# One order of work for another in an adaLN block with dilated window attention and a token-mixing MLP: loads on two queues, idle matmuls and the first transposes

## The chip, the core and the metric

The kernel runs on one NeuronCore of one Trainium2 chip. The metric is the device time of one execution in microseconds (us), the median over several runs. Five engines take part: PE (TensorE, matmuls; PEld is its weight loads), DVE (VectorE), ACT (ScalarE), POOL (GpSimd) and SP (SyncE, which here only issues DMAs). Each engine takes its own instructions strictly in the order in which the program gives them, so a row that waits holds up everything behind it on that engine.

## What is computed

x is 2048 tokens by 512 channels (bfloat16). Cut to what matters, the reference is:

```python
mod = silu(c) @ w_mod                      # 6 rows of 512: sa ca ga sb cb gb
h = layernorm(x) * (1 + ca) + sa
qkv = h @ wqkv                             # 32 heads of 16
# every token s attends to s, s-2, s-4, ... s-14 (8 keys, earlier than 0 masked)
x = x + ga * (softmax(q . k / 4) . v) @ wo
h = layernorm(x) * (1 + cb) + sb
h = layernorm(h)                           # first step of the MLP
u = gelu(h.T @ w1 + b1)                    # mixes tokens: 2048 -> 1792, per channel
y = u @ w2 + b2                            # 1792 -> 2048
x = x + gb * y.T
```

## The kernel before

The 2048 tokens are 16 tiles of 128. The attention half works on five chunks of 2, 4, 4, 4 and 2 tiles (SIZES). In each chunk the layer norm statistics are taken on DVE (one bn_stats) or on ACT (two passes with an accumulator), the rows are normalised, turned to channels on partitions (by PE in chunks 0 and 1, by a transposing DMA in chunks 2 to 4), and multiplied by wqkv. DVE forms the products of q with the eight shifted k (`qk`, four per chunk), PE sums them over the heads' channels (`red`), then follow maximum, exponent and sum, and DVE forms the products with v (`pv`, four per chunk), which PE sums (`pvacc`). PE multiplies by wo and adds x with an identity matmul; second and third layer norm follow (`ln2`, `aff`, `ln3`, `h3`). The first MLP product (`mlp1`) accumulates over the 16 token tiles, and so can begin on the early tiles while later chunks are in attention; its partial sums are parked in SBUF (`park`) and brought back by a PE identity matmul (`inj`) or by a DVE addition. After GELU, `mlp2` gives the 16 output tiles one after the other; `fin` on DVE and a store end each.

**Who sets the order.** The kernel builds a list of some 790 named operations with their dependences, and the string ORDER names them in the order in which they are issued. Behind a colon stands the engine for operations that have a choice (`:a` ACT, `:d` DVE, `:p` POOL, `:s` SP); for matmuls `:q` splits one into four 32-column ones and `:n` leaves the identity matmul out (DVE adds instead). `fill:64` is a piece of idle matmuls: 64 units, that is 16 matmuls of the identity by itself with 512 columns, and one of 128 columns for each unit left over; nobody reads their result. Token by token, `schedule` picks engine, PSUM bank and buffer.

**Names that the change and the steps below touch.** All of them are in the one kernel function.

- `ident` and `consts` (POOL): the identity matrix, and the group and mask constants. PE's first matmul needs the identity.
- `act_table` (ACT): loading the activation table. `ld_c`, `cps`, `silu_exp`, `silu_dve`: the condition row c is loaded, turned to a column by PE, and silu is taken on ACT and DVE, giving `sc`.
- `ld_x1`, `ld_x0`, `ld_x_1_2`, `ld_x_1_4`: token tiles of chunk 0 (one each) and the two tile pairs of chunk 1.
- `ln1s`, `ln1v`, `rstd1`, `nb1`, `n1`: statistics, variance, reciprocal deviation, offset and normalised rows of the first layer norm.
- `modcols1` (16 one-column matmuls of w_mod by sc) and `a1col` (DVE): the columns 1 + ca, the "scale columns". `hT0`, `hT1` (ACT or DVE): copies of the transposed tokens out of PSUM, multiplied by `a1col`. `tr0_0`, `tr1_0`, `tr1_2` are the transposes in front of them.
- `qkv0_02` and following: the first products with wqkv; `modcols0`, `sab`, `qvb0`, `qvb_cp0`: the offsets that sa brings to q; `ev0`: eviction of q and k; `qk0`: the first products of q and k on DVE.

Of loads that may go by SP's or ACT's queue, the helper is:

```python
QS = (("sp", nc.sync), ("act", nc.scalar))
def dma2(out_ap, in_ap, nbytes, writes, name):
    return G.add_any([(n_, 0.5, lambda q_=q_: q_.dma_start(out_ap, in_ap)) for n_, q_ in QS], writes=writes, name=name, ...)
```

The kernel's own numbers such as `0.5` are planning costs; with ORDER written out they decide nothing.

Of the kernel before, what the change touches and what calls it, by code (L numbers as in the profile page):

```python
# [196 lines left out]
qkv0_00 qvb0 wsc0_0:p ev0_10:a ld_b2 ld_wo1 hT1_1:d qkv1_00 ln1s11:d ln1s10:d ln1s13:d qkv1_10:q ln1v11 ln1v10
qvb_cp0:a ev0_00:a ln1s12:a ev0_02:d qkv1_13 ld_wqkv2 qkv0_20 ln1v13 qk0_3 qk0_2 ev1_13:a qk0_0 qvb1 ln1v12 qkv0_22:q
ld_wrow0 red0_0 ev1_00:a qkv1_03:q ev1_10:a qk0_1 red0_1 red0_2 red0_3 mask qvb_cp1:a ev0_20:a ev0_22:a wsc1_2:p
halo_v1:a qk1_0 ev1_03:a wsc1_3:a qkv1_11:q ld_wmod2 wsc2_3:a modrow0 ld_b1 mrows0:a ev1_11:a ld_wrow2 qkv1_02 max0  # L200
wsc0_2:p ld_wo0 n1_7:p sub0 rstd1_3 qkv1_01 ld_wo2 exp0 qkv1_12:q wsc1_1:p esum0:q qk1_3 red1_0 ev1_01:a qk1_1
ev1_02:a biascols n1_6:p ld_wrow1 rcp0 smB0 ev1_12:a ld_x_4_14 ln1s14:a qkv1_22 qk1_2 a2_0_2:a xt6 ld_wrow3 modrow1
red1_1 a2_0_1:a n1_9:p wsc2_0:d ln1s15:a ln1v14 nb1_3 n1_11:a qkv1_23:q mrows1 qkv1_21 ev1_21:a red1_2 red1_3 xt8
ev1_23:a fill:1 n1_10:p qkv1_20 ev1_20:a ev1_22:a qkv2_13 qkv2_10 wsc0_1:p vd0_2 ev2_13:a ln1v15 vd0_1 max1 sub1
qkv2_00 exp1 a2_0_0:s a2_0_3:s pv0_1 vd0_0 pv0_0 st_row0 pv0_2 qkv2_03 esum1:q ld_wo3 pvacc0_0 vd0_3 halo_v2:p
biascols_cp:a pvacc0_1 pv0_3 pvacc0_2 pvacc0_3 ev2_10:a ev2_00:a qk2_0 n1_13:a n1_12:a ld_row0 woq_s rcp1 smB1
# [5 lines left out]
qkv3_02:q ev3_00:a pv1_3 ev3_02:a pvacc1_0 ev3_20:a qkv3_01:q ev3_01:a qkv3_11:q xt14 ld_row1 n2_1:p vd2_3 pvacc1_1
smB2 aff0 qk3_0 vd2_1 fill:1 vd2_0 oev1_0:a oev1_1:a pvacc1_3 ev3_11:a qk3_1 qkv3_23:q oev1_3:a a2_2_2:s ln3s1:a
qkv3_03:q wo4 a2_2_1:s qk3_2 a2_2_0:s ev3_03:a ev3_23:a x1_4:a ln2q4:a wo2 x1_2:a a2_2_3:s red3_0 wo3:q x1_3:a ln2q3:a
qkv3_21:q ev3_21:a wo5 red3_1 pv2_3 x1_5:a vd2_2 qk3_3 qkv4_20:q red3_2 qkv4_22 red3_3 qkv4_12 fill:18 ln2q5:a
ld_w1_0_512 ln2q2:a ln2m2 pv2_0 pvacc2_0 vd3_0 ev4_20:a ln3s0:a ln3v0 ev4_12:a rstd2_2 ev4_22:a ln3v1 qkv4_02 oev2_0:a
ln2m4 rstd2_4 nb2_2 n2_2:a max3 sub3:q exp3 pvacc2_3 oev2_3:a qkv4_10:q pv2_2 vd3_2 esum3 nb2_4 pv2_1 vd3_1 n2_3:p
ld_w1_0_0 n2_5:a rcp3 smB3 pvacc2_2 fill:14 a2_3_0:s a2_3_1:s a2_3_3:s n2_4:a qkv4_00:q oev2_2:a rstd3_0 aff2 pvacc2_1
oev2_1:a wo6 wo9 wo7 aff4 nb3_0 ln3s2:d ev4_02:a ln3s3:a ln3v3 h3_1:p wo8 a2_3_2:s ev4_00:a ln3v2 ld_w2_0 ln3s4:d
rstd3_2 nb3_2 x1_9:a ln3s5:a h3_0:p mlp1_0_6_0:q x1_7:a ln3v4 x1_8:a h3_3:d mlp1_0_1_0 h3_2:d mlp1_0_6_2 mlp1_0_1_2  # L220
pv3_1 mlp1_0_5_0:q ln3v5 ev4_10:a ld_w1_0_896 x1_6:a mlp1_0_3_0:q mlp1_0_3_2:q ln2q7:a pvacc3_1 rstd3_4 mlp1_0_5_2:q
# [15 lines left out]
ld_w2_4 mlp1_1_0_10 ln3v14 ln3v12 rstd3_12 h3_11:a mlp1_1_6_10 inj1_5:n mlp1_1_5_6 mlp1_1_5_10 rstd3_14 mlp1_1_1_10
aff15 nb3_12 ln3s15:d ln3v15 h3_12:p nb3_14 park1_0:+ h3_13:p rstd3_15 nb3_15 inj1_2:n mlp1_1_2_6 ld_w1_1_896 h3_14:p
h3_15:a ld_w1_2_0 park1_1:+ mlp1_1_2_10 park1_2:+ mlp1_1_7_10 park1_3:+ park1_4:+ park1_5:+ mlp1_1_8_10 mlp1_1_10_10
park1_6:+ padd1_7 padd1_10 gelu10 padd1_8 mlp1_1_9_10 padd1_9 gelu9 mlp1_2_4_11 mlp1_2_4_14 mlp1_2_1_11 mlp1_2_1_14  # L240
padd2_1 padd2_4 gelu7 mlp1_2_0_11 mlp1_2_0_14 padd2_0 gelu0 mlp1_2_2_11 gelu4 gelu8 mlp1_2_2_14 ld_w1_1_1408
mlp1_2_3_11 mlp1_2_3_14 padd2_3 gelu3 ld_w1_2_640 mlp1_2_6_11 padd2_6 gelu6 padd2_2 gelu2 mlp1_2_5_11 mlp1_1_11_10
padd1_11 mlp1_2_5_14 padd2_5 gelu1 gelu11 mlp1_1_12_10 ld_w2_5 ld_w2_7 mlp1_1_13_10 gelu5 mlp2_0_0 padd1_12 gelu12
mlp2_0_0b ld_w2_2 ld_w2_9 ld_w2_13 ld_w2_11 padd1_13 gelu13 mlp2_0_0c mlp2_6_0 mlp2_4_0 gsc fin0_0 st_out0_0 fin4_0
st_out4_0 mlp2_8_0 fin8_0 mlp2_3_0 fin3_0 mlp2_2_0 fin2_0 st_out2_0 mlp2_1_0 fin1_0 mlp2_7_0 st_out3_0 fin6_0
st_out6_0 fin7_0 mlp2_10_0 fin10_0 st_out7_0 mlp2_11_0 mlp2_5_0 st_out1_0 fin5_0 st_out5_0 mlp2_14_0 fin11_0
# [829 lines left out]
```

## Time and profile before

| what | us |
|---|---|
| time, median of 3 runs | 201.56 (201.33 to 201.79) |
| the profiled execution's own time | 202.11 |
| span of its profile | 200.4 |
| PE busy / DVE busy / ACT busy in the span | 191.0 / 159.6 / 128.6 |

The span runs from the first to the last instruction of the program; 1.7 us of the execution lie outside it. Every row of the profile carries line 142, the wrapper that issues all instructions, so rows are told apart by the tiles they write and read ("psS<-hT,wst" is a product of tokens with raw wqkv, "big<-q_sb,k_f" a `qk`, "big<-a2sb,vD" a `pv`, "psL<-big,group" a `red`). A timeline row gives start, length, engine, operation and tiles, the count of instructions merged in it, and in brackets the idle time before it and what ended that. Lengths of PE matmuls are from start to modelled end and overlap; their pace is read from the starts or from long rows.

### The profile page before, as it was taken

The numbers are of one execution on the slowest core, as the hardware profiler recorded it, in microseconds if no ns is written. First come the engines' busy times: TensorE is split into PE (matmuls) and PEld (weight loads), VectorE is DVE, ScalarE is ACT, GpSimd is POOL, SyncE is SP. The second block draws the span as 40 slices with busy tenths as digits, with TensorE's granted clock in tenths as the row PEclk, the third lists the DMA queues.
The fourth block names the chain that finished last, engine by engine and source line by source line (L and its number), as shares of the span: only waits on it lengthen the run. The fifth ranks groups of instructions, "written<-read, shape, count | busy, mean of one in ns | idle before, by whom it ended". The sixth has DMA issues, their size and how long they took to land.

```text
span 200.4 us, 4572 instructions
## 1 busy us (share of the span) xinstructions
PE 191.0 (95%) x1818; PEld 95.8 (48%) x1836; DVE 159.6 (80%) x241; ACT 128.6 (64%) x306; POOL 18.6 (9%) x45
## 2 busy tenths in 40 slices
...
GB/s 161 341 355 350 176 240 127 160 56 185 300 143 321 220 167 194 176 112 311 64 310 257 36 184 196 160 186 234 338 244 298 85 26 52 27 52 52 174 52 52
DMA packets 53889, 35.95 MB, mean 179 GB/s; under 512 B 24428, under 2 KB 50668, under 8 KB 53868
## 3 DMA queue, kind: packets, MB, share of 16 engines
...
q8 instruction: 14, 0.23, 0.5%
...
HBM read 22.55 MB, written 2.10 MB: 123 GB/s over the span
## 4 chain that ended last, share of the span: by engine, by line
PE 69%; DVE 22%; issue 4%; DMA 1%; ACT 1%; ACTq 0%; DVEq 0%
PE psS L142 67%; DVE big L142 14%; PE psL L142 3%; DVE st L142 2%; DVE h L142 2%; DMA c_t<-in_c_dram 1%; DVE mv L142 1%; ACT h L142 1%; DVE lsb L142 1%; DVE m L142 1%; DVE nb L142 0%; ACTq L142 0%; DVE woq L142 0%; DVE hT L142 0%; ACT rb L142 0%
## 5 line engine op out<-in xcount | busy, mean ns | idle before, releaser
L142 PEld LDWEIGHTS <-wst 128*128 128x128 bf16 (+1 forms) x536 | 34.9, 101 | 33.7 <-issue 4.0
L142 PE MATMUL psS<-h,wst 128*128 128x512 bf16 (+1 forms) x333 | 50.3, 380 | 0.5 <-issue 0.3
L142 DVE TENSOR_TENSOR big<-q_sb,k_f 128x4096 bf16<-128x4096 bf16 (+1 forms) x20 | 36.6, 1859 | 0.4 <-ACT q_sb L142 0.4
L142 DVE TENSOR_TENSOR big<-a2sb,vD 128x4096 bf16<-128x4096 bf16 (+1 forms) x20 | 36.5, 1860 | 0.2
L142 PE MATMUL psS<-hT,w_qkv 128*32 128x512 bf16 (+3 forms) x360 | 29.7, 346 | 0.0
L142 DVE SCALAR_TENSOR_TENSOR h<-psS,bcol,rows_bc 128x512 f32<-128x512 f32 (+2 forms) x17 | 12.1, 710 | 22.1 <-PE psS L142 20.6
L142 PEld LDWEIGHTS <-w_qkv 128*32 128x32 bf16 (+1 forms) x402 | 19.4, 109 | 17.8 <-issue 4.4
L142 PE MATMUL psS<-gT,big 128*128 128x512 bf16 x110 | 24.7, 379 | 0.1
L142 PEld LDWEIGHTS <-big 128*128 128x128 bf16 x144 | 12.0, 97 | 13.5
L142 ACT ACTIVATE junk<-xx 128x512 bf16<-128x512 bf16 x26 | 16.3, 627 | 3.3 <-DVE xx L142 1.4
L142 PE MATMUL psS<-woq,o_sb 128*32 128x512 bf16 (+1 forms) x107 | 15.7, 380 | 0.9 <-ACT o_sb L142 0.6
L142 ACT ACTIVATE gT<-psS,bcol 128x512 bf16<-128x512 f32 x14 | 9.0, 685 | 8.1 <-DVE psS L142 8.0
L142 POOL TENSOR_SCALAR h<-xx,rs,nb 128x512 bf16<-128x512 bf16 x9 | 6.9, 766 | 75.6 <-DVE nb L142 36.5
L142 DVE TENSOR_TENSOR psS<-psS,gT 128x512 f32<-128x512 f32 x14 | 9.3, 695 | 5.0 <-PE psS L142 5.0
L142 ACT ACTIVATE h<-xx,nb,rs 128x512 bf16<-128x512 bf16 x16 | 12.4, 808 | 0.5 <-DVE nb L142 0.4
L142 PEld LDWEIGHTS <-ident 128*32 128x32 bf16 (+1 forms) x137 | 7.0, 102 | 10.5 <-issue 5.9
L142 PE MATMUL psS<-ident 128*128 128x512 bf16 (+1 forms) x35 | 10.6, 450 | 1.4 <-POOL epscol L142 1.4
L142 PE MATMUL psS<-hT,wst 128*32 128x512 bf16 (+2 forms) x110 | 11.7, 352 | 0.1
L142 DVE TENSOR_TENSOR h<-h,xx 128x512 bf16<-128x512 f32 (+2 forms) x17 | 11.1, 653 | 0.6
L142 DVE TENSOR_TENSOR h<-h,rows_bc 128x1024 bf16<-128x1024 bf16 (+2 forms) x16 | 10.9, 689 | 0.4
L142 DVE BATCH_NORM_STATS2 st<-xx 128x6 f32<-128x512 bf16 x12 | 7.9, 680 | 3.9 <-DMA xx<-in_A_x_dram 3.8
L142 ACT ACTIVATE v_sb<-psS,qvb 128x512 bf16<-128x512 f32 (+1 forms) x20 | 11.0, 595 | 0.0
...
## 6 DMA issues: line engine op xcount, KB each, us to landing
...
```

The costliest lines, as they stand in the source:

```text
L142: r = fn(*a, **k)
```

## The change

The load of c gets the choice of queue that the token loads have, and ORDER is another list. Of the list, the head, the tokens spoken of below and the end are shown; the engines chosen for other operations change in 29 places.

```diff
-    add("act", 0.55, lambda: nc.scalar.dma_start(c_t[:], c[0].rearrange("(t p) -> t p", p=P)), writes=["c_t"],
-        name="ld_c", lat=2.0)
+    dma2(c_t[:], c[0].rearrange("(t p) -> t p", p=P), D * 4, ["c_t"], "ld_c")
...
-ident ld_x_1_2:a halo0 ld_c consts ld_x1:s ld_x0:s ld_x_1_4:s act_table ln1s3:d fill:4 cps ld_wmod1 silu_exp silu_dve
-fill:64 ln1s1:a ln1s2:a ln1s0:d ln1v1 ld_x_2_8 ln1v0 ln1s4:d ld_wqkv0 rstd1_0 nb1_0 n1_1:a fill:4 ln1v4 n1_0:p ln1s5:d
-ln1v2 ln1v5 ln1v3 rstd1_1 nb1_1 ld_x_2_6 modcols1 n1_2:d n1_5:d ln1s8:a a1col wsc0_3:p n1_4:d tr0_0 hT0_1:a hT0_3:a
-n1_3:d hT0_0:a fill:13 hT0_2:a ld_wqkv1 ld_wmod0 ln1s9:d ld_x_3_10 ln1s6:d tr1_0 tr1_2 hT1_2:a ln1v6 qkv0_02 ln1v9
+act_table ld_x1:s consts ld_c:a ident fill:13 ld_x_1_2:a cps silu_exp silu_dve ld_x0:s ln1s0:d ln1v0 ld_x_1_4:s
+ld_wmod1 ln1s1:a fill:70 ln1v1 rstd1_0 nb1_0 n1_0:p ln1s4:d ln1s5:d ln1s3:d ln1s2:a ln1v2 n1_1:a tr0_0 ln1v5 fill:7
+ld_x_2_6 ld_wqkv0 ln1v3 ln1v4 rstd1_1 nb1_1 n1_2:a n1_3:d n1_5:d modcols1 a1col wsc0_3:p hT0_1:a n1_4:d tr1_0 ld_wqkv1
+wsc0_0:p tr1_2 hT0_2:a hT0_0:a ln1s7:d ld_x_2_8 ln1s6:d ln1v6 wsc0_1:d wsc1_0:p fill:6 halo0 ld_wmod0 ld_x_3_10
+hT0_3:a qkv0_02 hT1_3:a ln1s9:d qkv0_10 hT1_0:a qkv0_12 modcols0 ln1s8:d hT1_1:a wsc1_1:p qkv0_00 ld_x_3_12 ld_wqkv2
...
-fill:1 ... fill:1 ... fill:18 ... fill:14          (pieces of idle matmuls in the attention half)
+fill:1 ... fill:9
...
-inj1_5:n
+inj1_5
...
-... mlp2_15_1 fin15_1 st_out15_1 mlp2_15_2 fin15_2 st_out15_2
+... mlp2_15_1 mlp2_15_2 fill:24 fin15_1 st_out15_1 fin15_2 st_out15_2
```

More of the change, by code (lines that the diff above doesn't have):

```diff
@@ L197 @@
[L197 to L206, printed above, removed]
@@ L212 @@
[L212 to L221, printed above, removed]
@@ L237 @@
[L237 to L246, printed above, removed]
@@ L247 @@
-st_out10_0 st_out11_0 ld_w2_15 fpre mlp2_9_0 mlp2_13_0 fin14_0 st_out14_0 st_out8_0 mlp2_12_0 fin9_0 st_out9_0 fin13_0
-st_out13_0 mlp2_15_0 fin12_0 st_out12_0 fin15_0 st_out15_0 mlp2_15_1 fin15_1 st_out15_1 mlp2_15_2 fin15_2 st_out15_2
+act_table ld_x1:s consts ld_c:a ident fill:13 ld_x_1_2:a cps silu_exp silu_dve ld_x0:s ln1s0:d ln1v0 ld_x_1_4:s
+ld_wmod1 ln1s1:a fill:70 ln1v1 rstd1_0 nb1_0 n1_0:p ln1s4:d ln1s5:d ln1s3:d ln1s2:a ln1v2 n1_1:a tr0_0 ln1v5 fill:7
+ld_x_2_6 ld_wqkv0 ln1v3 ln1v4 rstd1_1 nb1_1 n1_2:a n1_3:d n1_5:d modcols1 a1col wsc0_3:p hT0_1:a n1_4:d tr1_0 ld_wqkv1
@@ new lines @@
+wsc0_0:p tr1_2 hT0_2:a hT0_0:a ln1s7:d ld_x_2_8 ln1s6:d ln1v6 wsc0_1:d wsc1_0:p fill:6 halo0 ld_wmod0 ld_x_3_10
+hT0_3:a qkv0_02 hT1_3:a ln1s9:d qkv0_10 hT1_0:a qkv0_12 modcols0 ln1s8:d hT1_1:a wsc1_1:p qkv0_00 ld_x_3_12 ld_wqkv2
+ln1v7 ev0_10:a ln1v9 ln1v8 rstd1_2 sab:a qvb0 hT1_2:d qkv1_13:q ev0_12:a nb1_2 n1_9:a ln1s10:d ln1s13:d qvb_cp0:d
+ev0_02:a qkv1_00:q ln1s11:d ld_wrow0 ln1v10 ev0_00:a ln1s12:a ev1_00:a qkv1_03:q ln1v11 ln1v13 qkv0_20 qkv1_10
+ld_wrow2 ev1_03:a ld_wrow3 qvb1 n1_7:a ld_wo0 ld_wmod2 qk0_2 qk0_0 n1_6:p red0_0 qkv0_22:q qk0_3 qk0_1 red0_1
@@ new lines @@
+qkv1_11:q wsc0_2:p ev1_10:a red0_2 qk1_0 ld_b2 ld_wrow1 n1_8:p red0_3 mask ld_wo3 ln1v12 wsc2_2:a ld_x_4_14 max0
+ev1_13:a qk1_3 qkv1_01 xt6 qvb_cp1:a ev0_22:a ev0_20:a wsc1_2:a vd0_2 ev1_11:a sub0 exp0 vd0_3 fill:1 xt8 qkv1_02
+ev1_01:a esum0:q qk1_1 modrow1 rcp0 modrow0 ev1_02:a qkv1_12 mrows0:a st_row0 wsc2_0:a smB0 a2_0_3:s ev1_12:a qk1_2
+a2_0_0:s qkv1_21 wsc2_1:a ld_wo1 rstd1_3 a2_0_2:a a2_0_1:a ln1s14:a qkv1_22:q qkv1_23:q wsc1_3:a nb1_3 ev1_22:a
+n1_10:p mrows1 ln1s15:d ev1_23:a ln1v14 red1_0 red1_1 red1_2 red1_3 qkv1_20 vd0_1 qkv2_00 vd0_0 ld_row0 ev2_00:a max1
@@ new lines @@
+pv0_3 sub1 qkv2_11:q qkv2_10 exp1 esum1 n1_13:p halo_v1:a ev1_20:a qkv2_12 pv0_2 pvacc0_2 pv0_1 ev1_21:a rcp1 ev2_10:a
+ev2_11:a wsc2_3:a ev2_12:a qkv2_03:q ev2_03:a pv0_0 ld_b1 pvacc0_0 smB1 ln1v15 qkv2_01:q ev2_01:a ld_wo2 n1_11:p xt10
+pvacc0_3 pvacc0_1 oev0_0:a qkv2_02:q ev2_02:a qkv2_13:q halo_v2:p vd1_3 oev0_2:a qkv2_23 qk2_0 qkv2_22 n1_12:a woq_s
+wo0:q ev2_22:a qk2_1 rstd1_4 a2_1_3:s red2_0 ev2_13:a x1_0:a qk2_2 ln2q0:a vd1_2 wo1:q x1_1:a qk2_3 a2_1_2:s red2_1
+qkv2_21:q xt12 qkv3_11:q ln2q1:a ln2m0 nb1_4 qkv3_02:q a2_1_0:s a2_1_1:s pv1_2 ev3_11:a ev2_21:a rstd2_0 nb2_0 n1_15:a
@@ new lines @@
+red2_2 red2_3 ev3_02:a st_row1 qkv3_10:q ev3_10:a pvacc1_2 oev1_2:a ev2_23:a vd1_0 max2 qkv3_13 qkv2_20 sub2:q ld_row1
+n1_14:a vd1_1 halo_k3:a ev2_20:a qkv3_00:q exp2 pv1_0 pvacc1_0 oev1_0:a qkv3_12:q qkv3_21:q vd2_0 pv1_3 pvacc1_3
+ev3_00:a esum2 qkv3_03:q ev3_21:a xt14 n2_1:p pv1_1 n2_0:a aff0 ev3_13:a pvacc1_1 oev1_3:a vd2_2 qkv3_01:q ev3_03:a
+qk3_0 oev1_1:a wo3:q wo4:q rcp2 wo5 smB2 ev3_12:a qkv3_20:q ln3s0:a qkv4_10 qk3_3 x1_4:a ev3_01:a qk3_1 vd2_3 qk3_2
+ln3s1:a x1_5:a ln2q4:a wo2 ld_w1_0_512 ln2q5:a a2_2_2:s x1_3:a ln2q3:a x1_2:a a2_2_0:s qkv3_23:q red3_0 a2_2_1:s
@@ new lines @@
+halo_v3:a qkv4_02 ln2q2:a a2_2_3:s ev3_20:a red3_1 ln2m4 red3_2 rstd2_4 ev3_23:a pv2_3 vd2_1 qkv4_22:q ev4_22:a
+ld_w1_0_896 nb2_4 n2_5:a qkv3_22 ev3_22:a ln2m2 rstd2_2 qkv4_20:q halo_v4:p biascols biascols_cp:a pv2_0 ld_w1_0_0
+red3_3 vd3_1 ev4_02:a vd3_3 nb2_2 vd3_2 n2_2:a max3 fill:9 pvacc2_0 sub3 ev4_10:a pvacc2_3 n2_4:a pv2_2 exp3 qkv4_12
+pv2_1 ev4_20:a vd4_0 ld_w2_2 esum3 rcp3 pvacc2_2 smB3 a2_3_2:s oev2_2:a a2_3_3:s qkv4_00 ev4_12:a oev2_3:a oev2_0:a
+ln3v0 pvacc2_1 oev2_1:a wo7 a2_3_1:s n2_3:p ln3v1 ev4_00:a wo6 aff2 rstd3_0 aff4 wo9 wo8 nb3_0 ln3s2:d a2_3_0:s
@@ new lines @@
+ln3s3:a x1_6:a h3_1:p h3_0:p mlp1_0_5_0 mlp1_0_6_0 ln3v3 ln3v2 rstd3_2 ln3s4:d x1_7:a nb3_2 h3_3:a ln3s5:a ln3v4
+h3_2:d x1_9:a mlp1_0_1_0 ln2q6:a x1_8:a pv3_1 ln3v5 mlp1_0_1_2 rstd3_4 mlp1_0_6_2 mlp1_0_3_0 vd3_0 pv3_0 mlp1_0_3_2:q
+pvacc3_1 oev3_1:a mlp1_0_5_2:q nb3_4 mlp1_0_0_0:q mlp1_0_2_0 mlp1_0_2_2:q mlp1_0_0_2:q qk4_2 pv3_2 h3_5:a h3_4:a
+mlp1_0_2_4:q mlp1_0_0_4:q mlp1_0_1_4:q mlp1_0_3_4:q pv3_3 mlp1_0_6_4:q ln2q7:a ln2q8:a park0_0:a park0_1:a ln2q9:a
+ln2m6 park0_2:a ld_w2_3 mlp1_0_5_4:q pvacc3_2 oev3_2:a pvacc3_0 qk4_3 park0_3:a mlp1_0_8_0:q mlp1_0_8_2:q pvacc3_3
@@ new lines @@
+rstd2_6 nb2_6 oev3_0:a qk4_0 mlp1_0_4_0:q mlp1_0_4_2:q mlp1_0_4_4:q oev3_3:a wo12:q ld_w1_0_1152 wo13:qn red4_0 n2_9:a
+vd4_2 n2_8:a n2_6:a n2_7:d qk4_1 red4_1 x1_12:a red4_2 red4_3 park0_4:a mlp1_0_7_0:q park0_5:a aff6 ln2q12:a max4
+mlp1_0_10_0 mlp1_0_10_2 ln3s8:d ln3s6:d ln3s7:a ln3v7 wo11 x1_11:a park0_6:a ln3s9:d mlp1_0_7_2 mlp1_0_7_4 ln3v6 ln3v8
+ln3v9 sub4 exp4 rstd3_6 mlp1_0_8_4 x1_13:d nb3_6 ln2q13:a mlp1_0_9_0 mlp1_0_9_2 ld_w1_0_1408 vd4_1 mlp1_0_12_0
+mlp1_0_12_2 mlp1_0_10_4 h3_6:p esum4 rcp4 vd4_3 ln2m12 h3_7:d h3_9:d smB4 rstd2_12 wo10:n a2_4_3:s h3_8:d ln2q11:a
@@ new lines @@
+nb2_12 a2_4_1:a n2_13:p a2_4_2:a mlp1_0_9_4 x1_10:d n2_12:a ln2q10:d ln2m10 aff12 mlp1_0_12_4 mlp1_0_7_6 mlp1_0_8_6
+park0_7:a mlp1_0_9_6 mlp1_0_11_0 mlp1_0_10_6 rstd2_10 mlp1_0_12_6 a2_4_0:s park0_8:a park0_9:a nb2_10 inj1_5
+mlp1_0_11_2 n2_11:a ln3s13:a pv4_2 mlp1_0_11_4 park0_10:a pv4_0 pvacc4_0 mlp1_0_11_6:q n2_10:a ld_w1_0_1664 pv4_1
+pvacc4_1 oev4_0:a pvacc4_2 mlp1_0_13_0:q pv4_3 pvacc4_3 inj1_3:qn aff10 ln3s11:d park0_11:a mlp1_0_13_2 mlp1_0_13_4
+ld_w1_1_0 oev4_2:a wo14 x1_14 wo15 mlp1_0_13_6 ld_w1_1_640 mlp1_1_3_6 mlp1_1_5_6 ln3s10:a ln3v10 ln3v11 rstd3_10
@@ new lines @@
+park0_12:a ln2s14 ln2v14 x1_15 inj1_6:qn mlp1_1_6_6 rstd2_14 ld_w1_1_896 nb2_14 n2_14:p inj1_0:n ln2s15 mlp1_1_0_6
+inj1_1:n mlp1_1_1_6 ln2v15 aff14 ln3s12:a nb3_10 rstd2_15 nb2_15 h3_10:a mlp1_1_3_10 park0_13:a n2_15:p mlp1_1_5_10
+mlp1_1_6_10 ln3s14:d ln3v14 mlp1_1_1_10 ln3v12 ln3v13 rstd3_12 aff15 nb3_12 h3_13:p mlp1_1_0_10 rstd3_14 h3_11:p
+ln3s15:d ld_w2_0 h3_12:a ln3v15 park1_0:+ ld_w1_2_0 nb3_14 rstd3_15 nb3_15 inj1_4:n mlp1_1_4_6 park1_1:+ mlp1_1_4_10
+inj1_2:n mlp1_1_2_6 mlp1_1_2_10 ld_w1_1_1408 h3_15:d park1_2:+ h3_14:a mlp1_1_10_10 mlp1_1_8_10 ld_w2_4 park1_3:+
@@ new lines @@
+park1_4:+ park1_5:a park1_6:+ fpre mlp1_1_9_10 padd1_9 mlp1_1_7_10 padd1_7 ld_w1_2_640 mlp1_2_1_11 gelu9 gelu7
+mlp1_2_1_14 ld_w2_1 mlp1_2_4_11 padd2_1 mlp1_2_0_11 gelu1 padd1_8 gelu8 mlp1_1_11_10 padd1_11 gelu11 padd1_10 gelu10
+mlp1_2_0_14 mlp1_2_4_14 padd2_4 mlp1_2_2_11 mlp1_2_2_14 padd2_2 mlp1_2_3_11 ld_w2_5 padd2_0 mlp1_2_3_14 padd2_3 gelu4
+mlp1_2_6_11 padd2_6 gelu3 gelu2 mlp1_2_5_11 mlp1_2_5_14 padd2_5 mlp1_1_12_10 padd1_12 gelu0 gelu5 mlp1_1_13_10
+padd1_13 gelu6 gelu12 mlp2_0_0 mlp2_0_0b gelu13 mlp2_1_0 fin1_0 gsc mlp2_2_0 fin2_0 mlp2_0_0c mlp2_4_0 ld_w2_7 ld_w2_9
```

26 lines of the change are left out of this document (5 added, 21 removed).

## The prediction, made before the changed kernel ran

> **What bounds the kernel now.** I read the page first, then the chain of work that ended last, then busy time by stretches, and then the timeline of the first 26 us, where most of the change lies. The page and, below it, pieces of the chain (start, length, what):
>
> ```profile
> PE 191.0 (95%) x1818; PEld 95.8 (48%) x1836; DVE 159.6 (80%) x241; ACT 128.6 (64%) x306; POOL 18.6 (9%) x45
> ```
> ```profile
> 1.33 2.60 DMA c_t<-in_c_dram
> ...
> 3.98 7.09 PE psS L142 x34
> ...
> 11.10 0.16 DVE a1col L142
> 11.26 1.02 DVE h L142 x2
> ...
> 56.29 10.16 PE psS L142 x141
> ...
> 69.33 5.71 DVE big L142 x3
> ...
> 102.95 1.14 DVE big L142
> ...
> 144.85 10.74 PE psS L142 x49
> ...
> 197.36 0.29 DVE h L142
> ```
>
> The chain begins with the load of c, runs over PE's idle matmuls, a1col and two normalised rows, goes to and fro between PE and DVE until 104 us, and is PE's alone from there to the end. The long piece gives PE's pace: 10.74 / 49 = 0.219 us for a matmul of 512 columns. The stretches (length, then busy PE, PEld, DVE, ACT, POOL) say which of the two is the limit:
>
> ```profile
> 18.80:104.10 85.30, 83.12 (x1197) 42.45 (x1198) 84.28 (x86) 79.88 (x191) 5.23 (x8) 1.00 0.67 194
> 104.10:197.10 93.00, 92.39 (x490) 43.77 (x499) 62.95 (x118) 34.67 (x82) 4.57 (x6) 1.00 0.54 148
> ```
>
> Between its first `qk` (18.80) and the end of its last (104.1) DVE is idle for 85.30 - 84.28 = 1.02 us in all. So the time is: start of the first `qk`, plus DVE's work up to the last `qk`, plus PE's work behind it, plus a fixed end. I work out what the change does to each.
>
> **Part 1, the start.** The rows of the timeline that carry it:
>
> ```profile
> 0.81 0.20 POOL L142 MEMSET ident<- 128x128 bf16 x1 [0.29 <-POOLq L1060]
> 0.82 0.48 ACTq L142 DMA_DIRECT2D xx<-in_A_x_dram  x1
> 1.32 0.10 POOL L142 MEMSET epscol<- 128x1 f32 x1
> 1.33 0.61 ACTq L142 DMA_DIRECT2D c_t<-in_c_dram  x1
> 1.52 0.12 POOL L142 MEMSET group<- 128x32 bf16 x1
> 1.98 1.28 ACT L142 ACT_TABLE_LOAD   x1 [1.98 <-issue]
> 2.94 0.29 POOL L142 TENSOR_SCALAR_AFFINE_SELECT nident<-nident 128x128 bf16<-128x128 bf16 x1
> 3.98 0.18 PE L142 MATMUL psS<-ident,c_t 4*128 4x4 bf16 x1 [1.94 <-DMA c_t<-in_c_dram]
> 4.10 6.58 PE L142 MATMUL psS<-ident 128*128 128x512 bf16 x17
> 4.27 0.62 ACT L142 ACTIVATE junk<-xx 128x512 bf16<-128x512 bf16 x1
> 7.90 0.81 ACT L142 ACTIVATE h<-xx,nb,rs 128x512 bf16<-128x512 bf16 x1 [0.23 <-DVE nb L142]
> 8.77 0.15 PEld L142 LDWEIGHTS <-ident 128*128 128x128 bf16 x1 [0.28 <-issue]
> 9.19 0.15 PEld L142 LDWEIGHTS <-ident 128*128 128x128 bf16 x1 [0.28 <-issue]
> 9.62 0.57 PEld L142 LDWEIGHTS <-ident 128*128 128x128 bf16 x3 [0.28 <-issue]
> 10.52 0.54 PE L142 MATMUL psS<-sc,big 128*128 128x1 bf16 x16
> 10.92 0.61 PE L142 MATMUL psS<-ident,h 128*128 128x128 bf16 x8
> 11.10 0.16 DVE L142 TENSOR_SCALAR a1col<-psS 128x4 f32<-128x4 f32 x1 [0.66 <-PE psS L142]
> 11.57 1.57 ACT L142 ACTIVATE hT<-psS,a1col 128x256 bf16<-128x256 bf16 x4 [0.73 <-PE psS L142]
> 12.07 1.28 PE L142 MATMUL psS<-ident,h 128*128 128x128 bf16 x16
> 13.19 2.78 PE L142 MATMUL psS<-hT,wst 128*128 128x256 bf16 x24
> ```
>
> Before: the idle matmuls come every 0.43 us until about 9.6 and at double pace from there; they end at 10.5, and the first product with wqkv starts at 13.19.
>
> After, in order. POOL makes the constants (1.52 to 2.94 + 0.29 = 3.23, so 1.71 us) ahead of the identity (0.81 to 1.42, so 0.61): 0.81 + 1.71 + 0.61 = 3.13 for PE's first matmul, where it was 1.43. ACT loads its table first: c is issued at 0.82 + 1.28 = 2.10 where it was 1.33, and lands 2.65 later (1.33 to 3.98) at 4.75. The new piece of 13 units (3 wide matmuls and a narrow one, 1.4 us) hides that wait. The token pair that was first on ACT's queue now starts at about 2.7; its first reader comes at 7.2, so 4 us of other work hide the later load. Behind c's column, 70 units are 17.5 wide matmuls from 4.87 on.
>
> The double pace came 9.6 - 4.1 = 5.5 us into steady matmuls. By the same distance it comes at 3.13 + 5.5 = 8.65: (8.65 - 4.87) / 0.427 = 8.9 slow ones, then 8.6 x 0.219 = 1.9 us: end at 10.55, as before (10.5). What follows is longer. The first transposes (0.45) and the piece of 7 (one wide, three narrow: 0.38) now stand ahead of modcols1 (10.92 - 10.52 = 0.40, and 0.18 until a1col): a1col starts at 10.55 + 1.41 = 11.95, where it was 11.10. Its copies cannot begin earlier by the swap, for `hT0` multiplies by a1col; and `n1_4` stands behind a1col on DVE, so the transposes of chunk 1 wait for it as well: 11.95 + 0.16 + 0.37 = 12.5, 16 transposes 0.9, the piece of 6 0.33: first product at 13.75. ACT agrees: a1col's end 12.1 + 1.57 = 13.7. That is **+0.56**. Behind it the kernel runs the same six steps to the first `qk` (three products, modcols0, product, qvb0), so 18.80 becomes 19.35.
>
> The ends: if the pace doubles at a fixed 9.6, 11.1 slow and 6.4 fast matmuls end at 11.0, +1.0. If it doubles much sooner, other things hold the start: ACT reaches its first statistics 0.77 later (4.27 to 5.04, with c), the row written by 7.90 + 0.81 = 8.71 ends at 9.5, a normalised row of chunk 1 follows at 10.7 to 11.5 on ACT, and the four copies end at 13.1: -0.1. I keep +0.56, range -0.1 to +1.0.
>
> [...]
>
> **Part 2, DVE from the first `qk` to the last.** The order of `qk` and `pv` hardly changes. Between these two points three operations differ: one weight scaling (0.35) and one `h3` row (0.41) leave DVE, and one bn_stats (0.68) comes:
>
> ```profile
> L142 DVE BATCH_NORM_STATS2 st<-xx 128x6 f32<-128x512 bf16 x12 | 7.9, 680 | 3.9 <-DMA xx<-in_A_x_dram 3.8
> L142 DVE TENSOR_SCALAR h<-h,rs,nb 128x512 bf16<-128x512 bf16 x5 | 1.9, 409 | 0.0
> L142 DVE TENSOR_SCALAR w_qkv<-h,a1col 128x512 bf16<-128x512 bf16 x1 | 0.3, 346 | 0.0
> ```
>
> 0.68 - 0.76 = **-0.08**. Waits are unknown: at best all 1.02 us of idle time go, at worst a new one as large comes (PE takes one more product of chunk 1, qkv1_11, four wide matmuls or 0.9 us, ahead of the matmuls that the maximum of chunk 0 waits for); I take 0 and keep both ends. The pieces of idle matmuls in this part shrink from 34 units to 10:
>
> ```profile
> 76.61 1.14 PE L142 MATMUL psS<-ident 128*128 128x512 bf16 x6
> ...
> 82.34 0.93 PE L142 MATMUL psS<-ident 128*128 128x512 bf16 x5
> ```
>
> At PE's pace 24 units are 6 wide matmuls, 1.3 us. They stand at the maximum of chunk 3, where PE waits for DVE; I cost them at nothing, as DVE's work is the same; -1.3 is the end if PE were last there.
>
> **Part 3, PE behind the last `qk`.** The same matmuls in another order, and inj1_5 on PE again where DVE added: one wide matmul, **+0.22**. The `:q` marks that come and go cost nothing: split or whole, the columns are the same. Two late weight blocks (ld_w2_11, ld_w2_15) stand behind stores on SP's queue, but five or more output tiles ahead of their readers, 14 x 0.219 = 3.1 us each. fill:24 (6 wide, 1.3 us) comes behind the last real matmul, while the last store is out:
>
> ```profile
> 196.38 0.94 PE L142 MATMUL psS<-woq,wst 128*128 128x128 bf16 x14
> ```
>
> It ends near 198.6, and the span at 200.4; without that cover it would cost at most 1.3.
>
> **Sum.** 0.56 - 0.08 + 0.22 = +0.7. The profiled execution took 202.11 (span 200.4 and 1.7 around it), so 202.8 by its own measure; it lay 0.55 above the median of the runs, 201.56, and so **202.2** as a median.
>
> **Rivals.**
>
> - *Idle time in the middle is won* (faster). If PE, not DVE, is last between 69 and 104 us, the 24 units count: 201.56 + 0.56 + 0.22 - 1.3 = 201.0; with the early start of part 1, 200.4. For it: PE is 83.1 of 85.3 us busy there, and the chain lies with PE for 10.16 us from 56.29. Against: the chain is DVE's from 69 to 104. It decides if DVE's idle time falls well below 1.02. Chance 0.26.
> - *The change does little of what it says.* c and one pair are on ACT's queue in both kernels, and a large idle piece is there in both; if the start is held by ACT (-0.1) and the rest repeats, 201.6. [...] Chance 0.20.
> - *Late clock or a new wait.* Pace doubling at 9.6 as before (+1.0 for the start), or DVE waiting some 0.5 us for evictions in chunks 0 and 1: 201.56 + 1.0 + 0.2 to 0.7 = 202.9. Against: steady matmuls begin 0.85 earlier. Chance 0.18.
> - The forecast, 202.2: chance 0.36.
>
> A measurement of this kernel tells about 0.2%, 0.4 us, from no change. Faster 0.26, same 0.20, slower 0.36 + 0.18 = 0.54. The range, 200.7 to 203.1, goes to most of the first rival and past the third; 0.2 stay outside.
>
> **What would show it.** a1col's start near 11.95 and the first wqkv product near 13.75 (13.1 and 14.2 are the ends); first `qk` near 19.35; DVE busy about 84 us from there to its last `qk`, idle time near 1; then 93 us of PE. It is wrong if the first `qk` starts at 18.8 or earlier, if DVE's idle time goes to near 0, or if PE shows waits behind 104 us that it did not have.

## The result, and the profile after

The changed kernel took 203.34 us (median of 6 runs, 202.48 to 203.93), the kernel before 201.49 on the same chip (6 runs, 201.25 to 201.79). The ratio is 1.0088, with a 95% interval of 1.0058 to 1.0117: slower by 1.85 us. The prediction said 202.2 and 200.7 to 203.1: the right direction, but 0.7 where 1.85 came.

The profiled execution took 202.48, with a span of 200.4. It was the quickest of the six; the other spans were 200.7 to 201.8. Its page shows almost the same busy times as before, with one block of instructions more (queue 8: 15 packets and 0.25 MB, so 16 to 17 KB each; before, 14 and 0.23 MB):

```profile
PE 192.1 (96%) x1890; PEld 96.8 (48%) x1890; DVE 158.6 (79%) x240; ACT 127.3 (64%) x302; POOL 19.3 (10%) x45
...
q8 instruction: 15, 0.25, 0.5%
```

Pieces of the chain of work that ended last (start, length, what). It no longer begins with the load of c: POOL's constants and then the identity start it and release PE at 3.09; then come DVE's statistics and a row on ACT.

```profile
2.74 0.29 POOL ident L142
...
3.09 1.70 PE psS L142 x5
...
5.67 0.61 DVE st L142
...
7.42 1.79 DVE st L142 x3
...
10.36 0.82 ACT h L142
...
11.54 10.77 PE psS L142 x157
```

The start, from the timeline (start, length, engine, operation, tiles):

```profile
0.81 1.28 ACT L142 ACT_TABLE_LOAD   x1 [0.81 <-PEq L1060]
0.84 0.57 ACTq L142 DMA_DIRECT2D c_t<-in_c_dram  x1
1.44 0.41 ACTq L142 DMA_DIRECT2D xx<-in_A_x_dram  x1
4.59 0.18 PE L142 MATMUL psS<-ident,c_t 4*128 4x4 bf16 x1
6.81 2.73 PEld L142 LDWEIGHTS <-ident 128*128 128x128 bf16 x13 [0.28 <-issue]
9.56 0.61 PE L142 MATMUL psS<-ident,h 128*128 128x128 bf16 x8
11.01 0.15 DVE L142 TENSOR_SCALAR a1col<-psS 128x4 f32<-128x4 f32 x1
12.66 2.78 PE L142 MATMUL psS<-hT,wst 128*128 128x256 bf16 x24
18.23 2.33 DVE L142 TENSOR_TENSOR big<-q_sb,k_f 128x2048 bf16<-128x2048 bf16 x2
```

In this one execution the start is earlier than before: first product at 12.66 (13.19 before), first `qk` at 18.23 (18.80). The pace doubled (from 0.43 to 0.22 us between the starts of wide matmuls) at 6.9 here, at 9.7 in the profile of before. The two stretches behind it, by the same view as before:

```profile
18.23:103.28 85.05, 82.69 (x1216) 42.41 (x1209) 84.28 (x87) 79.80 (x192) 6.61 (x9) 1.00 0.68 192
103.28:196.41 93.13, 93.06 (x524) 43.82 (x517) 62.50 (x119) 34.44 (x81) 4.59 (x6) 1.00 0.54 148
```

85.05 + 93.13 = 178.18, where it was 85.30 + 93.00 = 178.30. So up to the last real matmul this execution is 0.7 us ahead (196.41 against 197.10), and yet its span is the same 200.4. The 0.7 us is lost behind it. SP's two last stores, from SP's own timeline, first of the kernel before and then of the changed one:

```profile
197.35 0.33 SPq L142 DMA_DIRECT2D out_dram<-h  x1
197.78 0.38 SPq L142 DMA_DIRECT2D out_dram<-h  x1
```
```profile
196.67 1.05 SPq L142 DMA_DIRECT2D out_dram<-h  x1
197.82 0.38 SPq L142 DMA_DIRECT2D out_dram<-h  x1
```

The issue of the second-last store took 1.05 us, not 0.33, and the last store stands behind it on SP. The view of transfers, cut to 196.0 to 197.6, names what else moved then: besides the stores (queue 1), one block of instructions. Before, the last block moved from 181.84 to 183.15 us.

```profile
q1 hardware_dynamic: 265, 0.18, 35.9%
q8 instruction: 1, 0.02, 3.6%
```

And 202.48 - 200.4 = 2.08 us lie outside the span, where it was 202.11 - 200.4 = 1.7.

### The profile page after: what moved, and what is told of

It is laid out like the page before. It is cut to its first block, busy times and chain, and to the rows that moved or that the text cites. A ratio compares the mean times of both kernels' runs of the same rounds, so it can differ in the third digit from the quotient of the medians.

```text
span 200.4 us, 4688 instructions
## 1 busy us (share of the span) xinstructions
PE 192.1 (96%) x1890; PEld 96.8 (48%) x1890; DVE 158.6 (79%) x240; ACT 127.3 (64%) x302; POOL 19.3 (10%) x45
## 4 chain that ended last, share of the span: by engine, by line
PE 62%; DVE 26%; ACT 5%; issue 4%; POOL 1%; ACTq 0%; DVEq 0%; POOLq 0%
PE psS L142 60%; DVE big L142 17%; DVE h L142 4%; PE psL L142 2%; DVE st L142 2%; DVE mv L142 1%; ACT h L142 1%; DVE lsb L142 1%; ACT gT L142 1%; DVE nb L142 1%; ACT junk L142 1%; ACT lv L142 1%; DVE m L142 1%; ACT rs L142 1%; DVE ls L142 0%
## 5 line engine op out<-in xcount | busy, mean ns | idle before, releaser
L142 PE MATMUL psS<-h,wst 128*128 128x512 bf16 (+1 forms) x344 | 51.3, 379 | 0.3 <-ACT o_sb L142 0.3
L142 PEld LDWEIGHTS <-wst 128*128 128x128 bf16 (+1 forms) x542 | 35.4, 101 | 32.7 <-issue 2.6
L142 PE MATMUL psS<-woq,o_sb 128*32 128x512 bf16 (+1 forms) x136 | 16.7, 380 | 0.5 <-ACT o_sb L142 0.3
L142 ACT ACTIVATE h<-xx,nb,rs 128x512 bf16<-128x512 bf16 x17 | 13.5, 808 | 1.4 <-DVE xx L142 1.1
L142 ACT ACTIVATE junk<-xx 128x512 bf16<-128x512 bf16 x21 | 13.2, 626 | 1.6 <-issue 1.3
L142 POOL TENSOR_SCALAR h<-xx,rs,nb 128x512 bf16<-128x512 bf16 x11 | 8.4, 767 | 51.1 <-DVE nb L142 39.0
L142 PE MATMUL psS<-ident 128*128 128x512 bf16 (+1 forms) x40 | 10.0, 393 | 3.1 <-POOL epscol L142 3.1
L142 PEld LDWEIGHTS <-ident 128*128 128x128 bf16 (+2 forms) x125 | 7.1, 101 | 10.8 <-issue 3.6
L142 ACT ACTIVATE q_sb<-psS,qvb 128x512 bf16<-128x512 f32 (+1 forms) x20 | 11.3, 604 | 0.5 <-DVE qvb L142 0.2
```

What stands on the lines that cost most here:

```text
L142: r = fn(*a, **k)
```

## The experiments

Four theories go by letters in the first expectations: **A**, the moment at which PE's pace doubles varies from one execution to the next and carries the start with it; **B**, the middle varies; **C**, the program became so long that PE fetches a 15th block of instructions, which falls on the last stores; **D**, chance, or the idle matmuls at the end themselves disturb the stores. Every edit is to ORDER alone. "First product" is the first with wqkv; the number of PE's instructions is counted in the program.

### The changed kernel again

No edit.

> The changed kernel once more, for a second profile and more times. Its six times lie in two groups, 202.5 to 202.9 and 203.8 to 203.9, with spans of 200.4 to 200.8 and 201.7 to 201.8. Theory A (the moment at which the matmul pace doubles differs between executions): the groups come again, and in a profile of the upper group the pace doubles near 10 us instead of 6.8, with the first wqkv product near 13.8 instead of 12.66. Theory B (the middle differs between executions): the start is the same in both groups and idle time of DVE differs by about 1 us.

Measured: 203.14 (202.74 to 203.57), ratio 1.0065 [1.0044, 1.0085]. In this profile the pace doubled at 9.04 instead of 6.89:

```profile
4.70 6.08 PE L142 MATMUL psS<-ident 128*128 128x512 bf16 x19
12.57 0.95 PE L142 MATMUL psS<-ident,h 128*128 128x128 bf16 x14 [0.45 <-DVE h L142]
13.69 0.49 PE L142 MATMUL psS<-hT,wst 128*128 128x256 bf16 x3
```

The idle piece behind c's column took 6.08 us (5.02 in the first profile), and the first product starts at 13.69. The first `qk` starts at 19.26, 1.03 later than in the first profile, and everything behind it is later by as much: 85.08 + 93.12 = 178.20 us up to the last real matmul, 178.18 before. So the start varies and the middle does not: A stands, B falls. The two groups of times did not come again: the six spans lie from 200.7 to 201.5 without a gap. The end is slow again, with a fetch at 198.0; this time it is the last store whose issue is long, 1.16 us instead of 0.38, while the one before it took 0.33:

```profile
198.14 1.16 SPq L142 DMA_DIRECT2D out_dram<-h  x1
```

### The idle piece in narrow matmuls, in both kernels

```diff
 (after)                             (before)
-fill:70                             -fill:64
+fill:3 (23 times) fill:1            +fill:3 (21 times) fill:1
```

The same idle time at the start in three times as many instructions; PE's program goes from 3782 to 3884 instructions in the one and from 3674 to 3770 in the other. fill:24 stays at the end of the changed one.

> The changed kernel with its 70 units of idle matmuls all as 128-column ones instead of 512-column ones: the same columns, but 102 more PE instructions ahead of the kernel's body. Theory C (the last 16 KB piece of PE's instructions is fetched at 196.4 us, while the last stores are issued, and holds SP's second last issue for 1.05 us instead of 0.33): the fetch comes some 10 us earlier, the last issues take 0.33 to 0.38 us again, and the span is 0.7 us shorter at the same start. Theory D (the slow issue is chance or comes of the idle matmuls at the end): the tail stays 0.7 us longer.

> The kernel before with its 64 units of idle matmuls as 128-column ones: the same columns, 96 more PE instructions, nearly as many as the changed kernel has. Theory C: a fifteenth fetch of instructions appears near the end, the last stores are held by about 0.7 us, and the time rises from 201.5 to about 202.2. Theory D: no fetch that matters, 201.5.

Measured: 203.88 (ratio 1.0094 [1.0072, 1.0116]) and 202.04 (1.0027 [1.0002, 1.0052]). In the narrow form of the changed kernel the 15th block comes at 189.5 instead of 196.4, the second-last store's issue is back at 0.33, and from the last real matmul to the end of the span it takes 3.27 us, as before (3.29), although the idle matmuls are still there. What was won is lost elsewhere: the 12th block moved to 115.0. The view of transfers from 113.3 to 117.5, and the one of the unedited changed kernel from 112.4 to 114.7, each with the last piece of the same small transfer:

```profile
q8 instruction: 1, 0.02, 1.8%
...
a2sb<-lsb SPq DMA_DIRECT2D x2, 32.0 KB, 4.1
```
```profile
a2sb<-lsb SPq DMA_DIRECT2D x1, 32.0 KB, 2.3
```

That transfer took 4.1 us instead of 2.3, DVE's product with v waited 1.1 us for it, and PE 1.0 for DVE. This is one profile; that the block made the transfer late is likely and not shown. The narrow form of the kernel before has 14 blocks still, so for it the expected collision did not come; its end is undisturbed (3.28).

### Without the idle matmuls at the end

```diff
-mlp2_15_1 mlp2_15_2 fill:24 fin15_1
+mlp2_15_1 mlp2_15_2 fin15_1
```

> The changed kernel without the last piece of 24 units (six matmuls of 512 columns behind the last real one). Theory C: 12 fewer PE instructions are hardly enough to move the fetch past the end, so it still meets the last stores, time as the changed kernel within 0.3. Theory D, second half (the idle matmuls themselves hold the end): the time falls by 0.7 to 1.1 us, and the time outside the span from 2.1 to 1.7.

Measured: 202.03 (201.75 to 203.37, 12 runs), ratio 1.0022 [1.0003, 1.0042], against 1.0065 for the whole changed kernel in the same series. PE's program is 12 instructions shorter (3770), there are 14 blocks and none after 170.8, and the stores go out as before:

```profile
196.80 0.33 SPq L142 DMA_DIRECT2D out_dram<-h  x1
```
```profile
197.23 0.38 SPq L142 DMA_DIRECT2D out_dram<-h  x1
```

The expectation took 12 instructions for hardly enough to move the block; they were enough to drop it. The difference of the ratios, 0.43%, is 0.87 us; the traces give 3.99 and 4.02 us behind the last real matmul with fill:24, 3.28 without.

### The idle matmuls at the end, put into the kernel before

```diff
-mlp2_15_2 fin15_2
+mlp2_15_2 fill:24 fin15_2
```

> The kernel before with fill:24 behind its last real matmul, nothing else. By the prediction (cover behind the last store): 201.4 to 201.6, as without it. Theory 'only the instruction fetch costs, not the idle matmuls': no 15th fetch (PE then has 12 instructions more than before, 84 fewer than in the variant with narrow idle matmuls, which had 14), last real matmul to span end 3.28, issue 0.33, median within 0.2 of 201.5. Rival 'the idle matmuls themselves disturb the last stores': 4.0 and 202.2.

Measured: 201.85 against 201.65, ratio 1.0011 [0.9996, 1.0026]. PE's program has 3686 instructions and 14 blocks; from the last real matmul (196.88) to the end of the span (200.17) it takes 3.29 us, and no store's issue is long:

```profile
q8 instruction: 14, 0.23, 0.5%
...
197.14 0.33 SPq L142 DMA_DIRECT2D out_dram<-h  x1
...
197.56 0.38 SPq L142 DMA_DIRECT2D out_dram<-h  x1
```

So the same idle matmuls cost nothing that can be measured where they bring no block: D falls and C stands.

### modcols1 and a1col ahead of the rows

```diff
-fill:70 ln1v1 rstd1_0 ... n1_5:d modcols1 a1col wsc0_3:p
+fill:70 modcols1 a1col ln1v1 rstd1_0 ... n1_5:d wsc0_3:p          (and no fill:24)
```

> The changed kernel without fill:24, and with modcols1 and a1col put straight behind fill:70, ahead of the first transposes. In the changed kernel and its two variants the stretch from the end of the idle piece to the first product with wqkv is 3.12 to 3.16 us (without fill:24: 9.68 to 12.80). Theory 'the swap costs': the transposes, the piece of 7 and modcols1 no longer stand ahead of a1col; a1col comes about 0.6 us behind the idle piece instead of 1.46, the stretch falls to about 2.5, the first product comes 0.6 us sooner and the median is near 201.4. Rival 'ScalarE and the rows hold it': the copies of the transposes wait for the rows anyway, the stretch stays at 3.0 or more, median 202.0.

Measured: 209.1, ratio 1.0386 [1.0362, 1.041], neither of the two. My edit put a1col on DVE ahead of ln1v1, and a1col waits for PE's columns until 9.83; so DVE, with statistics ready, waited 3.35 us, all rows of chunk 1 came late, and PE ran out of work (idle time and its releaser in brackets):

```profile
9.83 0.16 DVE L142 TENSOR_SCALAR a1col<-psS 128x4 f32<-128x4 f32 x1 [3.35 <-PE psS L142]
...
11.88 0.23 PE L142 MATMUL psS<-ident,h 128*128 128x128 bf16 x1 [2.08 <-POOL h L142]
...
12.88 0.76 PE L142 MATMUL psS<-ident,h 128*128 128x128 bf16 x7 [0.77 <-ACT h L142]
```

By stretches (length, then busy PE, PEld, DVE, ACT, POOL; then the granted clock):

```profile
6.30:9.80 3.50, 3.50 (x32) 1.84 (x30) 0.18 (x1) 0.04 (x1) 0.00 (x0) 1.00 1.06 357
9.80:13.10 3.30, 0.45 (x5) 0.32 (x6) 2.60 (x8) 2.54 (x7) 2.04 (x3) 1.00 1.09 373
13.10:19.90 6.80, 5.61 (x40) 4.13 (x38) 5.43 (x18) 4.61 (x10) 1.56 (x5) 0.50 1.08 353
```

Behind two short idle times of PE (2.1 and 0.8 us) the granted clock was 0.50 from 13.1 to 19.9; the first product came at 17.93 instead of 12.80. On the price of the swap itself this run says nothing.

### The table load behind the loads, and in front of them in the kernel before

```diff
 (after, no fill:24)                                   (before)
-act_table ld_x1:s ... ld_c:a ... ld_x_1_2:a cps       -ident ld_x_1_2:a ... act_table ln1s3:d
+ld_x1:s ... ld_c:a ... ld_x_1_2:a act_table cps       +act_table ident ld_x_1_2:a ... ln1s3:d
```

> The changed kernel without fill:24, ScalarE's table load moved from ahead of its two loads to behind them. Outside the span lie 2.05 to 2.13 us in the changed kernel and its variants, 1.69 to 1.77 in the kernel before. Theory 'the table load first makes it': own time minus span falls to about 1.72 and the median from 202.0 to 201.7. Rival 'something else (the order of the first GpSimd work, the stores, the length of the programs)': it stays at 2.05 or more, median 202.0. Loads: c was issued 0.84 in the changed kernel, during the table load; if that load does not hold the queue, c lands within 0.1 us of the same moment.

> The kernel before with ScalarE's table load as its first instruction, ahead of the two loads on its queue; nothing else. By the prediction's step (the load holds the queue) the token pair is issued at about 2.1 instead of 0.82 and c at 2.6, c lands near 5.2 and the first steps move; the time rises by 0 to 0.5. By what the trace of the changed kernel shows (c issued at 0.84 during the table load) both are issued as before and the start does not move. Outside the span: 2.05 and a median of 201.9 if the table load in front makes the 0.36 us, 1.72 and 201.6 if not.

Measured: 202.64 (ratio 1.0059 [1.0037, 1.0082]) and 201.64 (1.0006 [0.9993, 1.0019]). Outside the span 2.08 and 1.73: the table load does not make the 0.36 us. The first of the two shows no more than a late draw of the pace in its profile (8.07; first product 13.21); why its median lies 0.6 us above that of the run without fill:24 alone is not shown beyond that. The second shows on the timeline that the load holds no issue behind it:

```profile
0.81 1.28 ACT L142 ACT_TABLE_LOAD   x1 [0.81 <-PEq L1060]
0.85 0.46 ACTq L142 DMA_DIRECT2D xx<-in_A_x_dram  x1
1.35 0.61 ACTq L142 DMA_DIRECT2D c_t<-in_c_dram  x1
```

The pair and c are issued at 0.85 and 1.35, 0.03 and 0.02 later than without a table load in front, and PE reads c at 3.93 (3.98 before).

### The identity first

```diff
-act_table ld_x1:s consts ld_c:a ident fill:13
+ident act_table ld_x1:s consts ld_c:a fill:13
```

It was run without fill:24, and whole (with fill:24).

> The changed kernel without fill:24, the identity made ahead of the other constants, so that PE's first matmul starts near 1.4 us instead of 3.1. Theory 'the moment of the double pace varies by itself': PE waits for c at 4.6 as before, the double pace comes anywhere between about 6.8 and 9.7, the first wqkv product between 12.6 and 13.8, median 202.0 within 0.3. Rival 'a fixed distance from the first matmul': the double pace comes 1.7 us sooner, near 5.6, the idle piece ends by 8.9 and the time falls by up to 0.8, to 201.2. Outside the span: 1.72 if the order of GpSimd's first work made the 0.36 us, 2.05 to 2.13 if not.

> The changed kernel, whole, with the identity made ahead of GpSimd's other constants; fill:24 stays. If start and end add up: the start as in the same edit without fill:24 (first wqkv product near 12.0, against 12.7 to 13.7), the end as in the changed kernel (a 15th instruction fetch near 196, the second-last store's issue at 1.0 us or more instead of 0.33, 4.0 us from the last real matmul to the end of the span instead of 3.28), median 200.5 + 0.7 = 201.2. Rival 'the gain of 1.5 us was the quieter end and not the start': 202.5 or more.

Measured: without fill:24 200.49 (200.18 to 202.39, 12 runs), ratio 0.9963 [0.994, 0.9986], faster than both kernels. Whole, 201.62, ratio 0.9995 [0.9977, 1.0012]. The first of the two:

```profile
1.43 1.57 PE L142 MATMUL psS<-ident 128*128 128x512 bf16 x4 [1.43 <-POOL epscol L142]
2.93 0.18 PE L142 MATMUL psS<-ident,c_t 4*128 4x4 bf16 x1
...
11.96 2.24 PE L142 MATMUL psS<-hT,wst 128*128 128x256 bf16 x19
```

PE starts 1.66 us sooner, and c is there when the idle piece of 13 ends, at 2.93: my own expectation said that PE would wait for c until 4.6, and that was wrong. In the changed kernel PE reads c at 4.59 because it is late itself. The pace doubled at 7.22 in this profile and at 4.53 in the whole kernel's, which is neither a fixed moment nor a fixed distance from the first matmul. The end is as expected: with fill:24 a block is fetched at 194.6, the second-last issue is long, and 4.24 us lie behind the last real matmul (3.28 without it):

```profile
195.17 1.31 SPq L142 DMA_DIRECT2D out_dram<-h  x1
```

Outside the span stay 2.1 us in both.

### The identity first, and a shorter idle piece

```diff
-fill:70 ln1v1
+fill:58 ln1v1          (identity first, no fill:24)
```

> The changed kernel without fill:24, identity first, and the large idle piece 12 units shorter (fill:58; 3 wide matmuls, 0.66 us at full pace). Theory 'the idle piece holds the start': the first wqkv product moves from 11.96 to 11.3 and the median from 200.5 to 199.9. Rival 'the rows of chunk 1 hold it' (DVE and ScalarE write them at 9.2 to 10.8, and the transposes of chunk 1 wait for them at 10.84): first product at 11.8 or later, median 200.4 to 200.5; if PE then idles long enough to lose the double pace, as with modcols1 and a1col ahead of the rows, several us more.

Measured: 200.51 (200.23 to 200.71, 5 runs), ratio 0.9944 [0.9924, 0.9964]. The pace doubled at 5.87; the first product started at 11.00, the very moment at which it did in the whole kernel with the identity first (pace at 4.53, fill:70). The bracket shows what holds it:

```profile
8.70 0.81 ACT L142 ACTIVATE h<-xx,nb,rs 128x512 bf16<-128x512 bf16 x1 [0.23 <-DVE nb L142]
9.56 1.27 PE L142 MATMUL psS<-ident,h 128*128 128x128 bf16 x16 [0.54 <-ACT h L142]
```

So 11.0 is set by the rows of chunk 1, and neither a shorter piece nor an earlier pace brings more; with a later pace the idle piece sets it. By its ratio this is the quickest version found, though its interval overlaps that of the version with fill:70; it beats both kernels.

### One transfer back on ScalarE's queue

```diff
-a2_1_1:s
+a2_1_1:a          (identity first, no fill:24)
```

> The changed kernel without fill:24, identity first, and the transfer a2_1_1 back on ScalarE's queue, where the kernel before has it (SyncE then issues 104 transfers as before, not 105). Theory 'the extra transfer on SyncE's queue makes the 0.36 us outside the span': own time minus span falls from 2.1 to about 1.72, median 200.1. Rival: it stays at 2.05 to 2.13, median 200.5; then the cause stays open.

Measured: 206.82, ratio 1.0244 [1.0217, 1.027], and 2.04 us outside the span: the theory falls, and the edit cost 6.3 us that I had not expected at all. On SP the transfer was issued at 46.4 and its packets were through by 48.5. On ACT's queue it stood behind evictions and statistics:

```profile
48.75 0.62 ACTq L142 DMA_DIRECT2D a2sb<-lsb  x1
...
53.99 2.29 DVE L142 TENSOR_TENSOR big<-a2sb,vD 128x4096 bf16<-128x4096 bf16 x1 [3.44 <-DMA vD<-v_sb]
```

By then three large transfers (524, 384 and 524 KB, from 47.09, 48.20 and 48.61) had been issued ahead of it, and its packets moved only from 52.5 to 53.5 us. Every product with v needs all four pieces of a2; DVE waited 3.44 us, and PE behind it. The bracket misleads here: it names a vD transfer that landed at 53.61, but by ORDER that is `vd1_1`, while this first product, `pv1_2`, reads `vd1_2`, issued at 40.86; what it lacked was the piece of a2. By stretches:

```profile
52.45:56.34 3.89, 0.18 (x5) 0.00 (x1) 2.35 (x3) 0.99 (x2) 0.00 (x0) 0.82 0.16 48
56.34:61.80 5.46, 5.46 (x28) 1.58 (x32) 5.46 (x4) 2.71 (x5) 0.77 (x1) 0.50 0.00 0
61.80:70.00 8.20, 8.10 (x148) 3.99 (x144) 5.74 (x5) 7.13 (x14) 0.00 (x0) 1.00 0.87 257
```

In these 3.9 us PE was idle but for 0.18, the granted clock fell (0.82 on average), and it was 0.50 for another 5.5 us.

### Ten small operations back on their engines

```diff
-ln1s8:d ln1s15:d ln2q10:d h3_15:d h3_14:a n2_14:p h3_3:a n2_12:a qvb_cp0:d n1_2:a
+ln1s8:a ln1s15:a ln2q10:a h3_15:a h3_14:p n2_14:d h3_3:d n2_12:d qvb_cp0:a n1_2:d          (identity first, fill:58, no fill:24)
```

> The changed kernel without fill:24, identity first, fill:58, and ten small operations (two statistics of the first and one of the second normalisation, rows n1_2, n2_12, n2_14, h3_3, h3_14, h3_15, qvb_cp0) on the engine that had them before. Theory 'the lengths of VectorE's, ScalarE's and GpSimd's programs make the 0.36 us outside the span': own time minus span falls clearly below 2.05, toward 1.72. Rival: it stays at 2.05 to 2.13, and the cause stays open. The span itself may move by some tenths, by the engines' waits (198.1 without the ten); time 200.1 to 200.9.

Measured: 202.52, ratio 1.0055 [1.0038, 1.0071]; 202.05 - 200.01 = 2.04 us outside the span. The rival holds. The span itself grew by 1.9, more than expected, mostly since its first `qk` comes at 17.63 instead of 16.74 and DVE waits more between its first and last `qk` (1.26 us instead of 0.75).

## Why the prediction was right in direction and short in size

- **Start, +0.56: the right sign, at or above the upper end of what was measured, for a partly wrong reason.** PE's first matmul came at 3.09 (predicted 3.13). The step "ACT loads its table first: c is issued at 2.10" failed: c was issued at 0.84, during the table load. It made no difference, since PE was held by the identity: PE read c at 4.59 (4.75). First products of the changed kernel and its variants with an unchanged start came at 12.66, 12.80, 13.21 and 13.69, of the kernel before and its variants at 12.59, 12.99 and 13.19: means 13.09 and 12.92, with a scatter of 1.0 us. Two of the four lie under 13.1, the lower end of the working, where ACT was to hold the start. Drawn against the moment of the pace, the changed kernel's lie on one line (6.89 to 12.66, 9.04 to 13.69, so 0.48 us for 1 us). Before, it doubled at 9.3 on average of three, 5.3 from steady matmuls; at that distance from 3.09 the product comes at 13.4 against 12.9. So +0.2 by the means and up to +0.5. At the first `qk`, where the prediction counts, the means are 18.66 (18.23, 18.38, 18.78, 19.26) and 18.63 (18.49, 18.59, 18.80), so these few profiles alone cannot tell the term from nothing. The spans of all runs do better: with the middle (-0.1) and the end taken off, their means (200.05 for the 12 runs without fill:24 and 201.05 for the 6 of the repeat, against 199.97) give +0.2 and +0.5. The profile of before was a late draw and that of after an early one: the two alone would have shown the start with the wrong sign, and with it the sign of being wrong that the prediction names (first `qk` at 18.8 or earlier).
- **What "the distance" is.** It is not fixed: from the start of steady matmuls the doubling took 3.1 to 6.0 us. The recorded clock changes at 6.28, 13.11 and 19.93 in the run with modcols1 and a1col ahead of the rows, and at 7.18, 54.96 and 61.79 in the one with a transfer back on ScalarE's queue: steps of 6.83, 6.82 and 6.83, and 47.78. In the other traces with a record the full pace lasts 191.15 or 194.56 us. What sets these moments is not shown.
- **The swap in front of a1col** cost less than the 0.5 in the working: from the end of the idle piece to the first product 3.12 to 3.16 us, against 2.73 to 2.89 before, so some 0.3. Being late has another source: the identity behind the constants. Undone alone, it brought the first product to 11.96 and 11.00, and the ratio from 1.0022 to 0.9963 and from 1.0065 to 0.9995.
- **Middle, -0.08, and behind the last `qk`, +0.22: right within 0.15.** Measured -0.23 and +0.1; DVE's idle time went from 1.01 to 0.77. That the 24 idle units of the middle cost nothing fits this, but no run took them alone. The first rival (idle time in the middle is won) did not come; nor did the second. The third had the nearest number, 202.9, by a mechanism that is not the one found.
- **End: the step that failed.** The prediction put fill:24 at nothing, "while the last store is out". The matmuls are covered, as the kernel before with fill:24 shows (ratio 1.0011). What was not counted is their 12 instructions. PE's program grew to 3782; with 3770 instructions and fewer there are 14 blocks, with 3782 and more there are 15, and the 15th falls on the last stores: an issue of 1.05 to 1.31 us instead of 0.33 or 0.38 in all three profiles where a block falls there and in none of the others. That is +0.7 to +0.95 us. Of the 14 earlier blocks of the changed kernel 13 lie in the two stretches, where DVE is idle for 0.77 us up to its last `qk` and PE for 0.07 behind it: no such cost shows there. In each of the three profiles the long issue ends 0.36 to 0.37 us after the block is through (197.36, 198.93 and 196.11 us). But a block does not hold every store: while the 14th moved, from 170.63 to 171.51, a store's issue took its usual time:

```profile
170.91 0.33 SPq L142 DMA_DIRECT2D out_dram<-h  x1
```

So why a fetch by PE lengthens an issue on SP at the end is not shown; that the two go together there, and leave together, is.
- **Outside the span, +0.36: not foreseen and not settled.** The working took "1.7 around it" as fixed. It was 2.04 to 2.15 in nearly every profile of the changed kernel and its variants (2.32 in one) and 1.7 in those of the kernel before and its variants (1.88 in one). It is no matter of the profiled runs alone: 2.04 to 2.18 in all 12 runs of the changed kernel, 1.67 to 1.80 in all runs of the kernel before that were made beside the variants; single runs of some variants reach up to 3.4. It is not the table load, the identity's place, the extra transfer on SP, fill:24, the number of PE's instructions, or the ten operations given back. What makes it stays open.

The sum of what was measured: +0.2 to 0.5 (start) - 0.1 (middle) + 0.7 to 0.95 (end) + 0.36 (outside) = +1.2 to +1.7, against 1.85 in the first series and 1.5 in the second. The start is the least certain of the four, and the outside term has a size but no cause.
